# A mixer with chunked attention on one core: TensorE's instructions of batches 1 to 3 put in program order

## The chip, the cores and the metric

The kernel runs on one core of a Trainium2 chip. The metric is the time of one execution on the device, in microseconds. A core has five engines that run side by side, each with its own queue of instructions in a fixed order: PE (TensorE, matmuls; its weight loads are shown as PEld), DVE (VectorE), ACT (ScalarE), POOL (GpSimd) and SP (SyncE, which here issues DMAs). An instruction at the head of a queue waits on semaphores until what it needs is there, and everything behind it on that engine waits too.

## The reference

Four batches. Attention in chunks of 32 queries, each seeing 8 memory tokens and the keys from 16 ahead of the chunk to 8 behind it; then a mixer over tokens and over channels.

```python
for c in range(nc):                                   # q, k, v: 4 x 8 heads x 768 x 64, chunk 32
    k_full = concat(mem_k, k[:, :, l_start:r_end])     # 16 left, 8 right
    scores = scale * q_c @ k_full.T
    a = exp(scores - max(scores)); a = a / (sum(a) + 1e-09)
    out[:, :, c_start:c_end] = a @ v_full
...
x = out as [batch, 768, 512]
h = x.transpose(0, 2, 1) @ U @ V                       # rank 32, over tokens
u = x + h.transpose(0, 2, 1)
return u + relu(u @ w_ch1) @ w_ch2                     # 512 -> 2048 -> 512
```

## The kernel before

Everything is float32; TensorE multiplies in a format with fewer bits (fp32r), so each large operand is kept as two parts, high and low (names end in h and l: uh, ul, w1h, w1l, hh, hl), and a product is three passes. A batch has 768 tokens, two blocks of 384 (`blk`), each three tiles of 128 tokens (`TB`); the 2048 hidden channels are 16 groups `f` of 128 (`NF`).

The mixer of one block is a loop over f. `w1_step` (L1181) makes 12 matmuls of 128x384 into a PSUM bank ps_h: one group of hidden channels. ScalarE takes the relu as hh (L1189), VectorE the rest as hl (L1190). `w2_step` of the group before then adds to the three accumulators acc: six matmuls of 128x512 with hh (L1235), then three with hl (L1241). At the end `add_to_x` (L1197) adds acc to the tile x, which is sent out.

Batch 0 decodes the weights and does both blocks together; batch 1 is `ffn`, once for each block, and meanwhile makes sums of pieces of w1 (`keep_sums`, on POOL and DVE) and stores them (`save_sums`). Batches 2 and 3 are `sevens`: for each of 8 pairs of f, seven products of sums of w1 with sums of the turned tokens (six matmuls of 128x384 each, L1108, numbered 0 to 6) take the place of the eight w1 half steps; the sums of w1 come back by DMA, three ahead (`RING`). Results that are needed twice are kept by ScalarE (`keep`, L1129) and added to by VectorE (L1125). `hst` holds block 1's hidden groups, whose w2 steps end the batch with no products beside them. The turned tokens that the products take are made by `seven_u`: x is transposed on TensorE (L1049), copied (uc), and combined into bh/bl (products 0 and 1), t12h/t12l (2, 3), t34h/t34l (4, 5) and b22 (6), by casts on ACT (L1055) and subtractions on DVE (L1042; ta and tb are between).

The attention of batch b+1 runs during the mixer of batch b. It is a Python generator, `attention`, that yields after each "piece": loads, transposes of k and q (L484), 128x128 into ps_a; scores (L547), 64 small matmuls of 32x64 by 64 in the code and 128 in the trace, since a full float32 matmul is two instructions on the chip; exponentials (pt), their transposes (L601), the product with V (L620, "av", again 128 in the trace); tokens are three tiles T of 256. `regroup` (L433) lays out kn and qn on DVE for the transposes; `load_v` fills vb (L466, L473). After the last tile come U and V (L649, L877, L894).

What sets the order. A context `tc.manual_schedule(engines=FRONT)` with FRONT holding PE leaves TensorE's instructions in the order in which the code emits them. Before, it is opened ahead of batch 0 and closed in `following_pair`, at that batch's end. After that a scheduler, which simulates the engines, chooses among the instructions that its model finds ready; `tc.high_priority` draws some ahead. The order so chosen is fixed when the kernel is built. How many pieces have been emitted at which step of the mixer is set by `pcs` and `give()` (40 pieces), but on TensorE the scheduler puts their instructions where it will. Tile pools: a tag names a slot in SBUF, and whoever takes it next waits until its last reader is done. `up` holds uh and ul of the two blocks (tags uh, ul, uh1, ul1) and is closed, with the other pools of `plain`, by `other_pools()` between batches 1 and 2; the pools of `seven_u` take their room.

## Time and profile before

| | |
|---|---|
| three runs | 688.34, 688.49, 689.48 us; median 688.49 |
| profiled execution | 690.57 us, span 688.7 us, mean granted TensorE clock 0.987 |
| PE busy | 652.6 us, 95% of the span |
| PEld, DVE, ACT, POOL busy | 82%, 50%, 34%, 9% |
| chain that ended last | PE 84%, DVE 5%, SP's queue 4%, DMA 4% |

The profile is of one execution; its span goes from the first to the last instruction. In its rows L12 is line 12 of the kernel, out<-in names the tiles, and xN counts instructions. A row's duration is that of one instruction from issue to result; matmuls are pipelined, so that one which starts every 0.175 us lasts 0.34. What an instruction costs in a row of others is therefore read from starts, not from durations. Behind a row in brackets stands the idle time of its engine before it and what ended that. Lines move by the change: L1181 becomes L1205, L1108 becomes L1134, L1235 and L1241 become L1256 and L1262, L547, L601, L620 become L545, L599, L618, L484 becomes L486, L1042 and L1055 become L1054 and L1069, L1190 becomes L1214, L1197 becomes L1221.

### The profile page before, as it was taken

How to read it: one execution, taken by the hardware profiler on the slowest of the kernel's cores; microseconds unless marked ns; L12 is line 12 of the kernel's file. 1: busy time of each engine (PE TensorE's matmuls, PEld its weight loads, DVE VectorE, ACT ScalarE, POOL GpSimd, SP SyncE). 2: the span in 40 equal slices, each digit the busy share in tenths (PEclk: the TensorE clock that was granted, in tenths of full speed). 3: DMA queues.
4: the chain of work that ended last, by engine and by line, in shares of the span. 5: the costliest groups of instructions: out<-in, count | busy, mean ns of one | idle time of the engine just before them, and what ended most of it. 6: DMA issues, size and time to landing. Idle time of an engine off the chain costs nothing.

```text
span 688.7 us, 15153 instructions
## 1 busy us (share of the span) xinstructions
PE 652.6 (95%) x6184; PEld 562.0 (82%) x6188; DVE 344.9 (50%) x681; ACT 232.7 (34%) x574; POOL 63.0 (9%) x95
## 2 busy tenths in 40 slices
PE   7686999998998899999999979999999999999997
PEld 4455999997877599888879969898878889899886
DVE  5857787899454532436433463253256731222322
ACT  4525335335521234333221433333224621112221
POOL 2000000022003033302431100000000000000000
PEclk9998999999999999999999999999999999999999
DMA  8888354453571398564744547767533125556301
GB/s 233 151 253 285 116 190 154 163 151 116 124 145 34 125 321 240 156 178 147 205 131 154 170 148 230 188 181 189 149 112 108 32 71 173 167 143 168 124 11 46
DMA packets 121548, 106.37 MB, mean 154 GB/s; under 512 B 51240, under 2 KB 91048, under 8 KB 121480
## 3 DMA queue, kind: packets, MB, share of 16 engines
q1 hardware_dynamic: 121480, 105.41, 52.6%
q8 instruction: 49, 0.80, 0.5%
q14 instruction: 19, 0.16, 0.1%
HBM read 79.30 MB, written 25.17 MB: 152 GB/s over the span
## 4 chain that ended last, share of the span: by engine, by line
PE 84%; DVE 5%; SPq 4%; DMA 4%; issue 2%; ACT 1%; DVEq 0%; ACTq 0%
PE acc L1235 22%; PE ps_h L1181 18%; PE ps_h L1108 18%; PE acc L1241 11%; DMA rw<-in_moe_w_ch_dram 3%; PE ps_a L484 2%; PE ps_a L620 2%; PE ps_a L547 2%; PE ps_a L1235 2%; SPq L466 1%; PE ps_a L601 1%; PE acc L1227 1%; SPq L298 1%; DVE x L1197 1%; PE ps_a L649 1%
## 5 line engine op out<-in xcount | busy, mean ns | idle before, releaser
L1235 PE MATMUL acc<-w,hh 128*128 128x512 f32 x606 | 160.1, 397 | 0.0
L1235 PEld LDWEIGHTS acc<-w,hh 128*128 128x128 f32 x606 | 111.6, 189 | 21.9 <-issue 1.8
L1181 PE MATMUL ps_h<-uh,w1h 128*128 128x384 f32 x252 | 86.7, 348 | 7.3 <-ACT w1h L338 6.6
L1241 PE MATMUL acc<-w,hl 128*128 128x512 f32 x303 | 88.0, 395 | 0.0
L1181 PE MATMUL ps_h<-ul,w1h 128*128 128x384 f32 x252 | 85.4, 341 | 0.1
L1190 DVE SCALAR_TENSOR_TENSOR hl<-ps_h,hh 128x384 fp32r<-128x384 f32 x63 | 34.9, 553 | 89.9 <-ACT hh L1189 89.8
L1189 ACT ACTIVATE hh<-ps_h 128x384 fp32r<-128x384 f32 x63 | 30.9, 490 | 120.3 <-PE ps_h L1181 120.2
L1241 PEld LDWEIGHTS acc<-w,hl 128*128 128x128 f32 x303 | 56.1, 188 | 10.6
L1181 PE MATMUL ps_h<-uh,w1l 128*128 128x384 f32 x252 | 56.3, 345 | 0.0
L1181 PEld LDWEIGHTS ps_h<-uh,w1h 128*128 128x128 f32 x252 | 47.5, 190 | 10.5 <-ACT w1h L338 6.9
L1181 PEld LDWEIGHTS ps_h<-ul,w1h 128*128 128x128 f32 x252 | 47.9, 190 | 2.9 <-DVE ul L979 0.4
L1181 PEld LDWEIGHTS ps_h<-uh,w1l 128*128 128x128 f32 x252 | 46.0, 192 | 0.0
L1125 DVE TENSOR_TENSOR hst<-ps_h,hst 128x384 f32<-128x384 f32 x32 | 17.8, 556 | 47.8 <-ACT hst L1129 44.8
L1108 PE MATMUL ps_h<-t34h,w1l 128*128 128x384 f32 x128 | 39.8, 352 | 0.0
L1108 PE MATMUL ps_h<-t12h,w1l 128*128 128x384 f32 x128 | 38.3, 355 | 0.0
L1108 PE MATMUL ps_h<-bh,w1l 128*128 128x384 f32 x128 | 36.9, 341 | 0.0
L1125 DVE TENSOR_TENSOR c<-ps_h,c 128x384 f32<-128x384 f32 x16 | 8.9, 556 | 49.4 <-PE ps_h L1108 49.4
L1118 DVE SCALAR_TENSOR_TENSOR hl<-hst,hh 128x384 fp32r<-128x384 f32 x32 | 17.7, 555 | 30.4 <-PE acc L1241 27.7
L1129 ACT COPY hst<-ps_h 128x384 f32<-128x384 f32 x32 | 15.3, 478 | 45.5 <-PE ps_h L1108 45.5
L1117 ACT ACTIVATE hh<-hst 128x384 fp32r<-128x384 f32 x32 | 16.8, 525 | 40.8 <-PE acc L1235 34.5
L1001 POOL TENSOR_TENSOR vb<-w1h,w1l 128x512 f32<-128x512 f32 x16 | 20.7, 1299 | 91.7 <-DMA w1l<-w1ld 89.3
L1108 PEld LDWEIGHTS ps_h<-t34h,w1l 128*128 128x128 f32 x128 | 23.6, 188 | 4.3 <-ACT hst L1129 2.5
(233 smaller groups left out, 1090.5 us busy)
## 6 DMA issues: line engine op xcount, KB each, us to landing
w1l<-w1s SPq DMA_DIRECT2D x112, 256.0 KB
w1l<-w1ld SPq DMA_DIRECT2D x35, 256.0 KB
w1s<-sums SPq DMA_DIRECT2D x32, 256.0 KB
rw<-in_moe_w_ch_dram SPq DMA_DIRECT2D x14, 512.0 KB
qraw<-in_q_dram SPq DMA_DIRECT2D x24, 256.0 KB
out_dram<-x SPq DMA_DIRECT2D x24, 256.0 KB
vb<-in_v_dram SPq DMA_DIRECT2D x56, 98.0 KB
raw<-in_moe_w_ch_dram SPq DMA_DIRECT2D x20, 256.0 KB
```

The costliest lines, as they stand in the source:

```text
L484: nc.tensor.transpose(out=psv[:, p, r, :], in_=half[:, r, 2 * p:2 * p + 2, :].rearrange("n h d -> n (h d)"), identity=ident,)
L1001: nc.gpsimd.tensor_tensor(out=v2 if odd else v1, in0=hi, in1=lo, op=ALU.add)
L1108: nc.tensor.matmul(out=ps[:, :TOK], lhsT=w_, rhs=u, start=(start and m == 0), stop=(m == 5), skip_group_check=True,)
L1117: nc.scalar.activation(out=hh, in_=c, func=AF.Relu)
L1118: nc.vector.scalar_tensor_tensor(out=hl, in0=c, scalar=0.0, in1=hh.bitcast(F32), op0=ALU.max, op1=ALU.subtract,)
L1125: nc.vector.tensor_tensor(out=out, in0=ps[:, :TOK], in1=in1, op=ALU.add)
L1129: nc.scalar.copy(out=out, in_=ps[:, :TOK])
L1181: nc.tensor.matmul(out=ph[:, :TOK], lhsT=w[:, c, :], rhs=u[c], start=(m == 0), stop=(m + 1 == len(parts)),)
L1189: nc.scalar.activation(out=hh, in_=ph[:, :TOK], func=AF.Relu)
L1190: nc.vector.scalar_tensor_tensor(out=hl, in0=ph[:, :TOK], scalar=0.0, in1=hh.bitcast(F32), op0=ALU.max, op1=ALU.subtract,)
L1235: nc.tensor.matmul(out=acc[tt], lhsT=h[:, sl], rhs=w, start=(begins and m == 0), stop=False,)
L1241: nc.tensor.matmul(out=acc[tt], lhsT=hl[:, sl], rhs=w2h[f], start=False, stop=ends is not None)
```

## The change

The number of instructions on each engine stays the same; their order changes, most of all on TensorE. The manual order is closed at the end of the kernel, so the order of batches 1 to 3 is that of the code too. Pieces are given by `pace(slots)`: one call of `give` after each w1 step and one inside each w2 step, between the six hh and the three hl matmuls (ffn, 55 slots), six calls a pair in `sevens` (52 slots). There are 49 pieces in place of 40; some of the added ones hold no instruction. `seven_u` and the making of uh and ul (`uT_parts`) become generators, whose steps are given after the attention's pieces (`coming`). The pool `up` stays open; bh and bl, and the first two tiles hst, take the slots of uh, ul, uh1 and ul1. tb is made directly behind ta. The sums of w1 in batch 1 are made in the other of the two blocks for each pair of f.

Cut to its core:

```diff
+NPIECE = 49
...
+    up = ctx.enter_context(tc.tile_pool(name="up", bufs=1))
     plain = ExitStack()
-    up = plain.enter_context(tc.tile_pool(name="up", bufs=1))
...
+                regroup(kraw, kn, "kn", 0)
+                yield
+                for n, _ in enumerate(zip(load_parts(1), turns(0))):
+                    if n == 3:
+                        regroup(kraw, kn, "kn", 1)
                     yield
...
     def seven_u(b):
-        pool = seven["u"]
-        half = lambda name: pool.tile([P, NCK, TOK], F32R, name=name)
-        bh, bl = half("bh"), half("bl")
+        half = lambda pool, name, tag: pool.tile([P, NCK, TOK], F32R, name=name, tag=tag)
+        bh, bl = half(up, "bh", "ul"), half(up, "bl", "uh")
...
+        for tt, sl in enumerate(cols):
+            with tc.high_priority(offset=HIGH):
                 c0.append(turned_x(0, tt))
                 parted(bh[:, :, sl], bl[:, :, sl], c0[tt])
+            yield
+        for tt, sl in enumerate(cols):
+            with tc.high_priority(offset=HIGH):
                 c1.append(turned_x(1, tt))
                 ta.append(slot([P, NCK, P], F32, "ta"))
...
+                tb.append(slot([P, NCK, P], F32, "tb"))
+                sub(tb[tt][:, a], c1[tt][:, z], c1[tt][:, a])
+                sub(tb[tt][:, z], c0[tt][:, z], ta[tt][:, z])
+            yield "turned"
+        with tc.high_priority(offset=HIGH):
+            if "u" not in seven:
+                other_pools()
+            pool = seven["u"]
...
             product(xb, 7 * p + 2, False)
             keep(c12, xb)
+            give()
             product(yb, 7 * p + 3, True)
             give()
             product(xb, 7 * p + 4, False)
...
-            w2_step(b, 0, 2 * p, 0, p == 0, None, *h1)
+            w2_step(b, 0, 2 * p, 0, p == 0, None, *h1, give)
...
-            if b + 1 == SEVEN and f // 2 % 2 == blk:
+            if f // 2 % 2 != blk:
+                if f % 2 == 0:
+                    save_sums()
                 keep_sums(f, w1l)
             elif f % 2:
                 save_sums()
-            for _ in range(pieces[f]):
-                next(gen[0], None)
+            give()
...
-                w2_step(b, blk, *prev)
+                w2_step(b, blk, *prev, give)
...
+    def pace(slots):
+        tried, given = [0], [0]
+
+        def give():
+            tried[0] += 1
+            if tried[0] > slots:
+                next(coming[0], None)
+                return
+            while given[0] < NPIECE * tried[0] // slots:
+                next(gen[0], None)
+                given[0] += 1
+
+        return give
...
-            manual.close()
...
+        coming[0] = seven_u(b + 1) if b + 1 < B else iter(())
...
+    manual.close()
```

Three places show what becomes of the order. The first is on TensorE, in batch 2, at the scores of the next batch's first tile (kall, qt), among the products (ps_h) and w2 steps (acc). Before:

```order
L547 MATMUL ps_a<-kall,qt 32x64 x3
L1108 MATMUL ps_h<-b_4896,w1l 128x384 x6
L547 MATMUL ps_a<-kall,qt 32x64 x12
L1235 MATMUL acc_5066<-w_1354,hh 128x512 x2
L1235 MATMUL acc_5067<-w_1354,hh 128x512 x2
L1235 MATMUL acc_5068<-w_1354,hh 128x512 x2
L547 MATMUL ps_a<-kall,qt 32x64
L1241 MATMUL acc_5066<-w_1354,hl 128x512
```

After:

```order
L1134 MATMUL ps_h<-t12l,w1l 128x384
L1134 MATMUL ps_h<-t12h,w1l 128x384 x2
L545 MATMUL ps_a<-kall,qt 32x64 x64
L1134 MATMUL ps_h<-t34h,w1l 128x384
L1134 MATMUL ps_h<-t34l,w1l 128x384
```

The 64 small matmuls of a tile's scores (128 in the trace), of which 3, 12 and 1 are seen here between larger ones, now stand in one row. Over batch 2 the scores stood in 14 such groups and av in 7, and now each in three; in batch 1 they stood in five and four, and now in three and three.

The second place is TensorE at the turn from batch 1 to batch 2: the last w2 steps of batch 1 (w2last) and products 0 to 3 of batch 2. Before:

```order
L1241 MATMUL acc_4167<-w2last,hl 128x512
L1235 MATMUL acc_4165<-w2last,hh 128x512 x2
L1235 MATMUL acc_4166<-w2last,hh 128x512 x2
L1235 MATMUL acc_4167<-w2last,hh 128x512 x2
L1108 MATMUL ps_h<-bh,w1l 128x384
L1241 MATMUL acc_4165<-w2last,hl 128x512
L1241 MATMUL acc_4166<-w2last,hl 128x512
L1241 MATMUL acc_4167<-w2last,hl 128x512
L1108 MATMUL ps_h<-bh,w1l 128x384
L1108 MATMUL ps_h<-bl,w1l 128x384
```

After:

```order
L1262 MATMUL acc_4188<-w2last,hl 128x512
L1256 MATMUL acc_4186<-w2last,hh 128x512 x2
L1256 MATMUL acc_4187<-w2last,hh 128x512 x2
L1256 MATMUL acc_4188<-w2last,hh 128x512 x2
L1262 MATMUL acc_4186<-w2last,hl 128x512
L1262 MATMUL acc_4187<-w2last,hl 128x512
L1262 MATMUL acc_4188<-w2last,hl 128x512
L1134 MATMUL ps_h<-bh,w1l 128x384
L1134 MATMUL ps_h<-bl,w1l 128x384
```

Products now begin behind the whole of the last w2 step, whose hl matmuls the queue reaches first; products 2 and 3 with t12 stand at the same distance behind.

The third is VectorE there. Before:

```order
L1042 TENSOR_TENSOR t12l<-ta,t12h 128x4x128 x2
L1042 TENSOR_TENSOR b_4896<-uc,b_4896 128x2x128
L1197 TENSOR_TENSOR x<-acc_4165,x 128x512
L1042 TENSOR_TENSOR b_4896<-uc,b_4896 128x2x128
L1197 TENSOR_TENSOR x<-acc_4166,x 128x512
L1042 TENSOR_TENSOR b_4896<-uc,b_4896 128x2x128
L1197 TENSOR_TENSOR x<-acc_4167,x 128x512
L1042 TENSOR_TENSOR t34l<-tb,t34h 128x4x128 x2
L1042 TENSOR_TENSOR t12l<-ta,t12h 128x4x128
```

After:

```order
L1054 TENSOR_TENSOR t12l<-ta,t12h 128x4x128 x3
L1054 TENSOR_TENSOR t34l<-tb,t34h 128x4x128 x2
L1054 TENSOR_TENSOR b_4954<-uc,b_4954 128x2x128 x2
L1054 TENSOR_TENSOR t34l<-tb,t34h 128x4x128
L1054 TENSOR_TENSOR b_4954<-uc,b_4954 128x2x128
L1214 SCALAR_TENSOR_TENSOR hl<-ps_h,hh 128x384
L1221 TENSOR_TENSOR x<-acc_4186,x 128x512
```

The third t12l, for which TensorE waited, now comes directly behind the other two; the last hl of batch 1 stands behind all nine subtractions, where it had stood ahead of them.

## The prediction

> **What bounds the kernel.** I read the page's totals and slices first, then the chain of waits, then busy times by stage, and last the timeline of TensorE inside the two stages that the change rewrites. From the page (engine totals; TensorE's slices and its granted clock; the chain by engine):

> ```profile
> PE 652.6 (95%) x6184; PEld 562.0 (82%) x6188; DVE 344.9 (50%) x681; ACT 232.7 (34%) x574; POOL 63.0 (9%) x95
> ...
> PE   7686999998998899999999979999999999999997
> PEclk9998999999999999999999999999999999999999
> ...
> PE 84%; DVE 5%; SPq 4%; DMA 4%; issue 2%; ACT 1%; DVEq 0%; ACTq 0%
> ```

> TensorE is busy for 95% and is 84% of the chain; the next engine, VectorE, is at half. The busy time by stage (window, length, busy time of PE, PEld, DVE, ACT, POOL with instruction counts, granted clock, DMA share, GB/s) shows batch 0, batch 1, the turn from batch 1 to 2, batch 2, and the rest:

> ```profile
> 0.00:232.10 232.10, 205.30 (x2476) 171.57 (x2481) 161.62 (x309) 94.53 (x241) 21.83 (x45) 0.97 0.56 157
> 236.10:397.60 161.50, 161.09 (x1568) 142.72 (x1569) 68.14 (x146) 51.73 (x136) 40.56 (x48) 1.00 0.62 190
> 397.60:409.50 11.90, 8.10 (x32) 6.90 (x31) 8.20 (x16) 3.44 (x7) 0.00 (x0) 0.86 0.43 114
> 409.50:549.00 139.50, 139.50 (x1439) 119.38 (x1438) 64.68 (x137) 51.42 (x126) 0.61 (x2) 1.00 0.55 155
> 549.00:688.70 139.70, 135.98 (x665) 120.12 (x663) 38.26 (x69) 28.78 (x59) 0.00 (x0) 1.00 0.38 111
> ```

> In batch 2 TensorE is never idle, so nothing can be had there by waiting less. But busy is not the same as moving at full rate, and the timeline shows where it does not. Start, duration, engine, line, tile: an iteration of batch 1 with nothing in it, then one with the 128 scores in a row, then one with the 128 products by V (av) in a row:

> ```profile
> 241.94 0.34 PE L1181 MATMUL ps_h<-uh,w1h 128*128 128x384 f32 x1
> 242.12 0.34 PE L1181 MATMUL ps_h<-ul,w1h 128*128 128x384 f32 x1
> ...
> 246.10 0.34 PE L1181 MATMUL ps_h<-uh,w1h 128*128 128x384 f32 x1
> ...
> 274.96 0.34 PE L1181 MATMUL ps_h<-uh,w1h 128*128 128x384 f32 x1
> ...
> 277.16 1.49 PE L547 MATMUL ps_a<-kall,qt 64*32 64x64 f32 x128
> ...
> 280.75 0.34 PE L1181 MATMUL ps_h<-uh,w1h 128*128 128x384 f32 x1
> ```

> The empty iteration takes 246.10 - 241.94 = 4.16 us: 12 matmuls every 0.175 us (242.12 less 241.94, rounded) and 9 every 0.227. With one run of 128 scores it takes 5.79, so that run costs 1.63.

> **The change, term by term.**

> Term 1, fewer fragments. Where the scheduler cuts the same scores up in batch 2, the timeline reads:

> ```profile
> 443.80 0.34 PE L1108 MATMUL ps_h<-bh,w1l 128*128 128x384 f32 x1
> ...
> 444.95 0.31 PE L547 MATMUL ps_a<-kall,qt 64*32 64x64 f32 x6
> 445.19 0.44 PE L1108 MATMUL ps_h<-bh,w1l 128*128 128x384 f32 x1
> 445.47 0.34 PE L1108 MATMUL ps_h<-bl,w1l 128*128 128x384 f32 x1
> ...
> 446.42 0.89 PE L547 MATMUL ps_a<-kall,qt 64*32 64x64 f32 x68
> 447.25 0.45 PE L1108 MATMUL ps_h<-t12h,w1l 128*128 128x384 f32 x1
> ```

> From 443.80 to 445.19 lie six large matmuls (1.05) and the six small ones (what the trace counts; the code's small matmuls are two each): 0.34 too much, and the matmul behind them takes 0.28 to the next instead of 0.175, another 0.105. So six small ones cost 0.445, and 128 in a row cost 1.63: a line through both is 0.387 for the switch and 9.7 ns for each small matmul. The run of 68 tests it: 447.25 - 445.19 - 6 x 0.175 - 0.105 + 0.105 (its own late successor) = 1.01, and the line gives 1.05. A run thus costs some 0.385 whatever its length. By the orders, batch 2 has its scores in 14 fragments and its av in 7; batch 1 has 5 and 4, since transposes stand inside. After, there are three and three in each: 15 + 3 = 18 fewer, 18 x 0.385 = 6.9. Bounds: 7.7 with the whole 0.43 that a run of two costs, and 0 if the cuts only fill holes (a rival). I take 6.9.

> Transposes go the other way: by the orders of batches 1 to 3, 13 joints between groups of four are opened. Two groups side by side, and then one, cost

> ```profile
> 250.94 0.34 PE L1181 MATMUL ps_h<-uh,w1h 128*128 128x384 f32 x1
> ...
> 256.01 0.34 PE L1181 MATMUL ps_h<-uh,w1h 128*128 128x384 f32 x1
> ...
> 260.64 0.34 PE L1181 MATMUL ps_h<-uh,w1h 128*128 128x384 f32 x1
> ```

> 5.07 - 4.16 = 0.91 for two and 4.63 - 4.16 = 0.47 for one: a joint saves 0.03, not 0.385, so opening 13 costs +0.4 (the bounds are 0 and 13 x 0.105 = 1.4, where each pays a whole late successor).

> Term 2, the turn from batch 1 to batch 2. TensorE, and VectorE at the same time:

> ```profile
> 400.08 0.44 PE L1108 MATMUL ps_h<-t12h,w1l 128*128 128x384 f32 x1
> 404.22 0.63 PE L1108 MATMUL ps_h<-t12l,w1l 128*128 128x384 f32 x1 [3.69 <-DVE t12l L1042]
> ...
> 407.80 1.54 PE L1235 MATMUL acc<-w,hh 128*128 128x512 f32 x6
> ```

> ```profile
> 397.94 0.42 DVE L1042 TENSOR_TENSOR tb<-uc,ta 128x256 f32<-128x256 f32 x1
> 398.27 1.28 DVE L1042 TENSOR_TENSOR t12l<-ta,t12h 128x512 fp32r<-128x512 f32 x2
> 399.48 0.42 DVE L1042 TENSOR_TENSOR b<-uc,b 128x256 fp32r<-128x256 f32 x1
> ```

> Product 1's 12 matmuls take 7.72 us here instead of 2.10, 5.6 too much; with the restarts ahead of it (395.4 to 400.1) I count 6.15. Of that 3.69 is the wait for the last t12l, and about 1.6 the matmuls behind it, eleven at 0.32 instead of 0.175. In the stretch behind the wait the granted clock is 0.53:

> ```profile
> 404.20:407.80 3.60, 3.58 (x11) 3.58 (x12) 1.60 (x3) 1.00 (x2) 0.00 (x0) 0.53 0.16 24
> ```

> [...]

> After, bh and bl lie in the pool that stays open, so products 0 and 1 no longer wait behind w2's last step. What is late next: VectorE now has three t12l, three t34l and three b22 ahead of the last hl (L1214), which w2's last step waits for, and TensorE waits in order. From the third tile's transposes to the need of hl lie 3 x 0.227 + 2.10 + 2.04 + 1.36 = 6.2 us of matmuls; VectorE needs, by spacing in its rows, 4 x 0.33 + 3 x 0.605 + 3 x 0.605 + 3 x 0.34 = 6.0, with ScalarE's copy (about 0.6) ahead and hl (0.55) behind, 7.1. So about 0.9 stays, with 0.5 for restarts 1.4. Bounds: 0.35 (no stall) and 4.15 (ta waits for slots that the stores of the sums free). I take 1.4: -4.75, range -2.0 to -5.8.

> Term 3, product 5 of each pair. Before, it stands behind only three w2 matmuls (0.68 us), while ScalarE must have emptied its bank:

> ```profile
> 576.87 0.86 PE L1241 MATMUL acc<-w,hl 128*128 128x512 f32 x3
> 577.60 0.44 PE L1108 MATMUL ps_h<-t34h,w1l 128*128 128x384 f32 x1
> 577.88 0.34 PE L1108 MATMUL ps_h<-t34l,w1l 128*128 128x384 f32 x1
> ```

> It starts 0.73 behind the first of them, 0.05 late, and its first matmul takes 0.28, 0.10 late: 0.15 for each of batch 3's 8 pairs, 1.2. After, all nine w2 matmuls stand there, 2.04 us. I take -1.1, between 0 and -1.2; in batch 2 most pairs have attention there, which term 1 has priced. Five products in a row also ask for their sums faster; I cost that at nothing: three sums are fetched ahead, and each product of cover is 1.05 us; without the cover it would be one wait of term 5's size.

> Term 4, the turn from batch 0 to 1: VectorE bound, as it stays; two g,v matmuls come later, out of a wait into the path: +0.2.

> Term 5, new waits. A fixed order waits where the scheduler would have put something else. Batch 0, already in a fixed order, shows the price, at its av runs:

> ```profile
> 196.67 0.92 PE L620 MATMUL ps_a<-vb,pT 64*32 64x64 f32 x62 [1.06 <-issue]
> 210.51 0.83 PE L620 MATMUL ps_a<-vb,pT 64*32 64x64 f32 x62 [1.05 <-issue]
> 214.05 0.45 PE L620 MATMUL ps_a<-vb,pT 64*32 64x64 f32 x28 [0.90 <-issue]
> ```

> ```profile
> L473 SPq DMA_DIRECT2D vb<-in_v_dram x4: 393/1046/1365, 180.0 to 204.1; - x4
> ```

> There the last loads of V are issued at 204.1, 5 to 10 us ahead of the last two waits. In the new order 18 to 22 us of matmuls stand between V's loads and the av run, so few such waits should come. Bounds: 0 (it cannot be below nothing, as the stretch of batch 2 has no idle to save) and twice batch 0's 3.0, 6.0. I take 1.5, half of one such set.

> What else moves costs nothing by its cover: the regrouping of q and k one piece earlier, and tb ahead of t12l, on VectorE at half load; the loads of q, k and V on SP's queue, with the DMA share at 0.55 in batch 2; the sums on POOL, at 9%, made in the other block of batch 1. Without that cover each would cost one piece's wait, about 1 us, and that is in term 5.

> Sum: -6.9 + 0.4 - 4.75 - 1.1 + 0.2 + 1.5 = -10.65. The profiled execution took 690.57 (span 688.70 and 1.87 around it), so 679.9; it stands 2.08 above the median of the three runs, 688.49. Against the median: **677.8 us**.

> **Rivals.**

> The other side: the fixed order waits. If each of the six score and six av runs, and the four or so transposes behind each exponential, waits once as in batch 0, at 1.05, ten waits undo the gain and more make it slower: 16 waits cost 16.8, less 12.15 of gains (the sum without term 5), 693.1. It decides at 12. Against it: V's lead of 18 us above. For it: batch 0, in a fixed order, is busy only 205.3 of 232.1, though its first part waits for weights. I give slower 0.11, and 0.19 to a middle case of 4 to 9 waits: 680 to 686.

> The cuts filled holes: where small matmuls stand between products, TensorE would otherwise have waited for a bank to be emptied. Then term 1 is nothing, and 684.7 follows. Against it: batch 3's products have no small matmuls between them and lose 0.15 a pair, not 0.385 a cut. I give 0.08, within the middle case's span.

> The clock falls in long runs. If 128 small matmuls did not count as work, each of the new whole runs would be followed by a slow stretch like that above, 1.6 us. The new order has 12 whole runs, of which 4 stood before: 8 x 1.6 = 13 us, so 690, no gain. Against it, the window of one of the four (the clock stands behind the five busy times):

> ```profile
> 276.90:278.60 1.70, 1.70 (x131) 1.35 (x129) 0.56 (x1) 0.71 (x2) 0.00 (x0) 1.00 0.50 55
> ```

> The clock stays at 1.00, and the large matmuls behind that run keep their rate (the iteration of 5.79), and so I give this 0.02. [...]

> The turn does not get shorter: if ta waits for its slots, term 2 is -2.0, 680.5; this lies in the forecast's own range.

> **How the numbers follow.** About 0.2% (1.4 us) is what a measurement of this kernel can tell from no change. Forecast, 673.5 to 680.5: 0.55. Middle case (waits or holes), 680.5 to 687: 0.27. The clock, 690: 0.02, half within 0.2%. Waits short of the whole gain, 687.1 to 689.9: 0.05. Slower by waits: 0.11. So faster 0.82, same 0.06, slower 0.12. The low end, 673.5, is the sum with term 1 at 7.7, term 2 at 5.8 and no waits (674.5), less 1.0 for sizes rounded in the rows; the high end, 687, takes in the middle case, and what is left out is 0.18 above and 0.02 below. The forecast's own range is 673.5 to 680.5.

> **What would show it.** Term 1: the timeline has L545 and L618 as x128 in one row each, and the stage from the turn to the end of batch 2 is some 5.5 us shorter with the same instructions. Term 2: the wait of 3.69 on t12l is gone, a wait of about 1 us on hl stands ahead of w2's last step in batch 1, and the clock there stays at 1.00. Term 3: product 5's first row in batch 3 reads 0.34. Term 5: the waits of TensorE have few new lines on L599, L618 or L545 in batches 1 and 2. The prediction is wrong if these waits sum to over 5 us, or if L1134 shows starts late by more after the runs were joined than before.

## The result, and the profile after

The changed kernel takes 682.13 us, median of 17 runs (678.34 to 685.91), against 689.48 for the kernel before in 17 runs beside them; the ratio is 0.9892, 95% interval 0.9869 to 0.9914. The forecast was 677.8, with a range of 673.5 to 687.0: faster, as forecast, by 7.4 us where 10.65 was forecast. The profiled execution took 685.91 us, the longest of the 17, which matters below.

The page's totals and chain read almost as before: the same 6184 matmuls, busy for the same share.

```profile
PE 648.7 (95%) x6184; PEld 563.7 (82%) x6188; DVE 345.2 (50%) x681; ACT 234.7 (34%) x574; POOL 63.0 (9%) x95
...
PE 86%; DVE 5%; SPq 3%; DMA 2%; issue 2%; ACT 1%; ACTq 0%; DVEq 0%
```

The list of TensorE's waits (what waited and for what: us in total, times, longest) no longer has the 3.7 on t12l; four of its lines are new or longer:

```profile
PE ps_h L1134 <- DMA w1l<-w1s: 2.5, 1, 2.5
...
PE ps_h L1205 <- DVE ul L997: 1.8, 1, 1.8
...
PE acc L1256 <- ACT hh L1213: 0.5, 1, 0.5
...
PE acc L1262 <- DVE hl L1214: 0.4, 1, 0.4
```

By stage (window, length, busy time of PE, PEld, DVE, ACT, POOL, clock, DMA share, GB/s): batch 0, batch 1, the turn from batch 1 to 2, the stretch behind it, the rest of batch 2, and the end.

```profile
0.00:233.10 233.10, 207.59 (x2476) 172.80 (x2481) 161.45 (x309) 94.50 (x241) 16.55 (x39) 0.96 0.55 156
237.00:396.40 159.40, 159.40 (x1558) 141.85 (x1559) 70.70 (x150) 54.27 (x141) 45.83 (x54) 0.99 0.63 191
396.40:412.00 15.60, 14.71 (x72) 12.52 (x71) 8.64 (x18) 3.62 (x9) 0.00 (x0) 1.00 0.59 180
412.00:419.00 7.00, 4.52 (x20) 4.04 (x19) 0.55 (x2) 0.48 (x1) 0.00 (x0) 0.78 0.91 249
419.00:545.00 126.00, 126.00 (x1390) 110.62 (x1390) 61.42 (x131) 51.58 (x123) 0.61 (x2) 1.00 0.54 144
545.00:683.80 138.80, 135.07 (x669) 121.16 (x667) 38.56 (x70) 28.62 (x59) 0.00 (x0) 0.99 0.38 116
```

The turn no longer holds an idle stretch of nearly 4 us. The next window does: 412 to 419 has 4.52 us of work in 7.00, at a clock of 0.78, with the DMA share at 0.91. That is a loss that the kernel before did not have.

To compare stages exactly, I number the 2592 large matmuls (w1 steps, products, w2 steps) of each trace in order of start; both kernels run the same number of them. The table gives, for each stretch of numbers, its length in a kernel's trace less its length in the trace of the kernel before, in us. A to F are numbers 670 to 700 (the turn from batch 0 to 1), 700 to 1330 (batch 1), 1330 to 1390 (the turn from 1 to 2), 1390 to 1450 (the stretch behind it), 1450 to 2020 (the rest of batch 2), 2020 to the end. A stretch with attention in it also shifts where a piece moves over its border, so D and E are best read together. Up to number 670 the code is the same, and its length alone differs from that in the trace of the kernel before by -2.8 to +1.9 in these traces; that is left out, and it is why the medians of single experiments, 6 runs each, settle less than the traces do.

| kernel | A | B | C | D | E | F | sum | median us | ratio to before (95%) |
|---|---|---|---|---|---|---|---|---|---|
| changed (its profile) | +1.99 | -1.37 | -4.56 | +5.51 | -6.38 | -1.16 | -5.97 | 682.13 | 0.9892 (0.9869 to 0.9914) |
| changed, again | +0.42 | -1.47 | -4.48 | +3.44 | -6.41 | -1.15 | -9.65 | 681.99 | 0.9900 (0.9858 to 0.9941) |
| g,v put back | +0.45 | -2.01 | -4.69 | +6.08 | -6.44 | -1.15 | -7.76 | 681.57 | 0.9891 (0.9851 to 0.9931) |
| stores later | +3.10 | -1.53 | -4.84 | +1.46 | -5.42 | -1.10 | -8.33 | 679.01 | 0.9849 (0.9817 to 0.9882) |
| both mended | +0.43 | -2.00 | -4.50 | +1.28 | -6.43 | -1.15 | -12.37 | 679.53 | 0.9849 (0.9817 to 0.9880) |
| loads later | +0.44 | -1.53 | -4.91 | +1.17 | -4.75 | -1.07 | -10.65 | 677.64, one run | |
| loads later, g,v back | +0.46 | -2.02 | -4.91 | +1.55 | -4.25 | -1.17 | -10.34 | 679.92 | 0.9861 (0.9831 to 0.9892) |
| all three | +0.46 | -1.92 | -4.86 | +0.42 | -4.36 | -1.15 | -11.41 | 680.51 | 0.9851 (0.9813 to 0.9888) |
| scores cut | +0.43 | +0.93 | -4.85 | +5.09 | -1.56 | -1.11 | -1.07 | 689.59 | 0.9997 (0.9974 to 1.0021) |
| scheduler's order | +0.25 | -1.74 | -6.13 | +5.37 | -2.39 | +0.68 | -3.96 | 686.20 | 0.9942 (0.9920 to 0.9963) |
| before, stores later | 0.00 | +0.12 | +0.10 | 0.00 | -0.09 | -0.33 | -0.20 | 689.88, one run | |

In TensorE's timeline after, the scores of a tile stand in one row, product 5 of a pair in batch 3 starts at full rate behind its w2 step (0.18 to the next, where the first matmul took 0.28 before), and the last w2 step of batch 1 waits twice:

```profile
435.91 1.48 PE L545 MATMUL ps_a<-kall,qt 64*32 64x64 f32 x128
437.32 0.44 PE L1134 MATMUL ps_h<-t34h,w1l 128*128 128x384 f32 x1
437.60 0.34 PE L1134 MATMUL ps_h<-t34l,w1l 128*128 128x384 f32 x1
...
573.10 0.84 PE L1262 MATMUL acc<-w,hl 128*128 128x512 f32 x3
573.78 0.34 PE L1134 MATMUL ps_h<-t34h,w1l 128*128 128x384 f32 x1
573.96 0.34 PE L1134 MATMUL ps_h<-t34l,w1l 128*128 128x384 f32 x1
```

```profile
397.73 1.66 PE L1256 MATMUL acc<-w2last,hh 128*128 128x512 f32 x6 [0.48 <-ACT hh L1213]
399.75 0.96 PE L1262 MATMUL acc<-w2last,hl 128*128 128x512 f32 x3 [0.36 <-DVE hl L1214]
400.55 0.34 PE L1134 MATMUL ps_h<-bh,w1l 128*128 128x384 f32 x1
```

So the gains came, and two losses stand beside them, in A and in D.

### The profile page after: what moved, and what is told of

Its sections match the earlier page's. It is cut to its first block, busy times and chain, and to the rows that moved or that the text cites. A ratio compares the mean times of both kernels' runs of the same rounds, so it can differ in the third digit from the quotient of the medians.

```text
span 683.8 us, 15135 instructions
## 1 busy us (share of the span) xinstructions
PE 648.7 (95%) x6184; PEld 563.7 (82%) x6188; DVE 345.2 (50%) x681; ACT 234.7 (34%) x574; POOL 63.0 (9%) x95
## 4 chain that ended last, share of the span: by engine, by line
PE 86%; DVE 5%; SPq 3%; DMA 2%; issue 2%; ACT 1%; ACTq 0%; DVEq 0%
PE acc L1256 22%; PE ps_h L1205 19%; PE ps_h L1134 18%; PE acc L1262 11%; PE ps_a L618 2%; PE ps_a L486 2%; PE ps_a L545 2%; PE ps_a L1256 2%; PE ps_a L599 1%; PE acc L641 1%; PE acc L1250 1%; PE ps_a L908 1%; DMA w1l<-w1s 1%; PE ps_a L647 1%; PE ps_a L1262 1%
## 5 line engine op out<-in xcount | busy, mean ns | idle before, releaser
L1214 DVE SCALAR_TENSOR_TENSOR hl<-ps_h,hh 128x384 fp32r<-128x384 f32 x63 | 35.0, 555 | 88.5 <-ACT hh L1213 88.4
L1134 PE MATMUL ps_h<-t34h,w1l 128*128 128x384 f32 x128 | 39.4, 349 | 0.0
L1134 PE MATMUL ps_h<-bh,w1l 128*128 128x384 f32 x128 | 36.7, 346 | 2.5 <-DMA w1l<-w1s 2.5
L1134 PE MATMUL ps_h<-t12h,w1l 128*128 128x384 f32 x128 | 37.4, 347 | 0.0
L1143 ACT ACTIVATE hh<-hst 128x384 fp32r<-128x384 f32 x32 | 16.8, 525 | 36.8 <-PE acc L1256 32.4
L910 DVE TENSOR_TENSOR x<-ps_a,x 128x512 f32<-128x512 f32 x24 | 16.4, 689 | 23.1 <-PE ps_a L908 23.1
L1134 PEld LDWEIGHTS ps_h<-bh,w1l 128*128 128x128 f32 x128 | 24.0, 192 | 3.4 <-issue 2.8
```

The source lines that it names most:

```text
L910: nc.vector.tensor_tensor(out=x, in0=hp, in1=x, op=ALU.add)
L1134: nc.tensor.matmul(out=ps[:, :TOK], lhsT=w_, rhs=u, start=(start and m == 0), stop=(m == 5), skip_group_check=True,)
L1143: nc.scalar.activation(out=hh, in_=c, func=AF.Relu)
L1214: nc.vector.scalar_tensor_tensor(out=hl, in0=ph[:, :TOK], scalar=0.0, in1=hh.bitcast(F32), op0=ALU.max, op1=ALU.subtract,)
```

## The experiments

**The loss in D: a sum of w1 that lands late.** Timeline of TensorE, and of SP's issues, in the changed kernel:

```profile
413.09 0.51 PE L1134 MATMUL ps_h<-bh,w1l 128*128 128x384 f32 x2
416.09 0.66 PE L1134 MATMUL ps_h<-bh,w1l 128*128 128x384 f32 x1 [2.48 <-DMA w1l<-w1s]
416.54 0.52 PE L1134 MATMUL ps_h<-bl,w1l 128*128 128x384 f32 x1
416.86 0.52 PE L1134 MATMUL ps_h<-bh,w1l 128*128 128x384 f32 x1
```

```profile
406.35 0.35 SPq L1118 DMA_DIRECT2D w1l<-w1s  x1
406.79 1.39 SPq L1231 DMA_DIRECT2D out_dram<-x  x3
408.27 2.01 SPq L425 DMA_DIRECT2D qraw<-in_q_dram  x2
410.38 1.05 SPq L1118 DMA_DIRECT2D w1l<-w1s  x2
```

Product 1 of the second pair waits 2.48 us for its sum, and the matmuls behind it go at a clock of 0.50 (415.97 to 419.38; 0.32 from start to start, where full clock has 0.175). Its sum, the ninth, is the first of the two issued from 410.38: it stands behind three stores of x (768 KB), two loads of q (512 KB) and k, and takes until 416.1. Theory: the wait on t12l had given the queue time for this. The first edit takes only the stores out of the way:

```diff
-            send()
+            if p > 1:
+                send()
```

> The changed kernel with the last three stores of x of batches 1 and 2 (256 KB each) issued behind product 4 of the third pair instead of the first. Theory (the removed wait had given the DMA queue time to drain, and now products reach a sum of w1 that is behind k, q and the stores on the queue): 768 KB less ahead of it, at the 0.3 to 0.4 MB per us moved there, lands the sum 1.9 to 2.5 us earlier; the wait of 2.48 us on w1l<-w1s falls under 0.6 and the half clock behind it goes, 3.5 to 4.5 us in all. Rival (the sum is late because its own slot is freed late): the wait stays within 0.5 us of 2.48 and the time does not change.

Measured: D falls from +5.51 to +1.46, 4.05 us less, and by 2.0 against the changed kernel's second trace (3.44), in which the wait was 1.94 with no half clock behind it. The wait on the ninth sum is gone, and with it the half clock. The 0.8 us on a sum that the list of waits still has (0.75 at 432.01) is another one, 18 us later, in E, and E is 1.0 worse (-5.42 against -6.38); in the second trace with this edit (both mended) there is none, and why it is here was not followed up. The ninth sum is issued 2 us earlier, 5.4 us ahead of the product that takes it, where it had been 3.2:

```profile
406.90 0.35 SPq L1118 DMA_DIRECT2D w1l<-w1s  x1
407.35 0.94 SPq L425 DMA_DIRECT2D qraw<-in_q_dram  x2
408.38 1.67 SPq L1118 DMA_DIRECT2D w1l<-w1s  x2
```

The rival falls, and the theory holds for this wait. But the stores had cost in two ways, the time in which SP issues them (1.39 us in the row at 406.79) and their 768 KB, and this run changes both. Two more runs ask whether it is the bytes or the stores as such, and whether the kernel before pays for them. In the first, `give()` is left out at three places of pair 0 and the stores stay:

```diff
-            give()
+            if p > 0:
+                give()
```

> The changed kernel with the first three pieces of attention in batch 2 (loads of k and q) three places later, the stores left where they are. Theory (what counts is the bytes ahead of the sum on the queue): 512 to 1024 KB less ahead of it, 1.4 to 2.5 us, so the wait of 2.5 us on w1l<-w1s is under 1 us and the half clock behind it is gone. Rival (only the stores matter, since they wait for the last adds to x on VectorE and hold up the queue of issues): the wait stays above 2 us.

The wait is 0.6 us, D is +1.17:

```profile
404.26 0.98 SPq L1118 DMA_DIRECT2D w1l<-w1s  x2
```

```profile
408.18 0.41 PE L1134 MATMUL ps_h<-bh,w1l 128*128 128x384 f32 x1 [0.57 <-DMA w1l<-w1s]
```

Here the ninth sum is issued 3.4 us ahead of its need, hardly more than the 3.2 of the changed kernel, but it is there 3.9 us after its issue, not 5.7 (5.1 in the second trace, 6.4 in the one with g,v put back): the bytes ahead of it count by themselves. But E is worse by 1.6 (-4.75 against -6.38). Of that 0.5 is an idle stretch ahead of scores at 459.7; the rest was not followed up.

The second is the kernel before, with the stores later:

> The kernel before with the last three stores of x of batches 1 and 2 issued two pairs later. Theory (before, the 3.7 us wait on t12l at the turn covers the queue, so that no product waits for its sums): the turn and the start of batch 2 keep their length within 0.5 us. Rival (the stores cost time there whatever stands before them): 2 us or more shorter.

C and D change by 0.1 and 0.0 us, as the theory had it. The rows of the kernel before say how the old wait covered the queue:

```profile
408.43 1.39 SPq L1207 DMA_DIRECT2D out_dram<-x  x3
409.92 0.55 SPq L423 DMA_DIRECT2D qraw<-in_q_dram  x1
410.56 0.76 SPq L1092 DMA_DIRECT2D w1l<-w1s  x1
```

```profile
415.97 0.69 PE L1108 MATMUL ps_h<-bh,w1l 128*128 128x384 f32 x3
416.50 0.34 PE L1108 MATMUL ps_h<-bl,w1l 128*128 128x384 f32 x1
```

The ninth sum is issued at 410.56 there, and the product that takes it begins with the third of the row's three matmuls, at 416.3, 5.8 us later. After, it is issued at almost the same time, 410.38, but TensorE, no longer held at t12l, is there at 413.6. Before, the sum was in time; now TensorE waits for the queue.

**The loss in A: two matmuls taken out of a hole.** In the changed kernel the first matmuls of batch 1 stand so (timeline, then two windows with their clock, the third number from the end):

```profile
234.75 0.44 PE L1205 MATMUL ps_h<-uh,w1h 128*128 128x384 f32 x1 [0.67 <-ACT uh L996]
237.00 0.44 PE L1205 MATMUL ps_h<-ul,w1h 128*128 128x384 f32 x1 [1.81 <-DVE ul L997]
...
239.46 0.53 PE L1205 MATMUL ps_h<-uh,w1h 128*128 128x384 f32 x1
239.78 0.53 PE L1205 MATMUL ps_h<-ul,w1h 128*128 128x384 f32 x1
```

```profile
235.07:238.48 3.41, 1.59 (x9) 1.48 (x9) 1.88 (x4) 0.00 (x0) 0.00 (x0) 1.00 0.97 348
238.48:241.89 3.41, 3.41 (x13) 3.41 (x12) 0.56 (x1) 0.49 (x1) 3.25 (x4) 0.50 0.90 224
```

Before, two g,v matmuls stood within the wait for ul:

```profile
234.75 1.10 PE L894 MATMUL ps_a<-g,v 96*128 96x512 f32 x2 [0.44 <-DVE ul L979]
```

The edit in `w1_step` puts them back:

```diff
+            if m == 0 and (b, blk, f) == (1, 0, 0):
+                next(late[0])
+                next(late[0])
```

> The changed kernel with two g,v matmuls put back behind the first matmul of batch 1, where the scheduler had them. Theory (the split idle time kept the clock): in the changed kernel TensorE stands idle 0.67 and 1.81 us at that turn and then runs some 3 us at a granted clock near 0.5; with the two matmuls in the hole the clock stays at 1.00 there and the stage from the last w2 step of batch 0 to the second w1 step of batch 1 is 1.5 to 2.0 us shorter. Rival (the two matmuls cost only their own 0.23 us each wherever they stand): the slow stretch stays and the stage is 0.2 to 0.5 us shorter.

In the trace, the clock stays at 1.00 and A is +0.45:

```profile
231.12 0.44 PE L1205 MATMUL ps_h<-uh,w1h 128*128 128x384 f32 x1 [0.68 <-ACT uh L996]
232.17 1.10 PE L908 MATMUL ps_a<-g,v 96*128 96x512 f32 x2 [0.61 <-DVE ul L997]
233.37 0.45 PE L1205 MATMUL ps_h<-ul,w1h 128*128 128x384 f32 x1
```

The median, 681.57, does not show it: the edit costs or gains less than its interval. What it wins in every trace lies in B: -2.01 here, and -1.92 to -2.02 in the other three traces with the two matmuls put back, against -1.37 to -1.53 where they stand later in batch 1. That is 0.5 us, close to the 0.23 us that each of the two takes. The repeat of the changed kernel tells why.

> The changed kernel itself on the same chip, as the measure for the other three. From the runs so far: 682 us, ratio 0.989. In its profile the wait on w1l<-w1s of 2.0 to 3.0 us in batch 2 must be there again (it follows from the order of the DMAs), while the stretch at half clock behind the turn from batch 0 to 1 may be there or not, if it depends on where a window of the clock's control falls.

It has the same 1.81 us of idle time, no slow stretch, and A of +0.42, as much as with the edit:

```profile
232.99 0.44 PE L1205 MATMUL ps_h<-uh,w1h 128*128 128x384 f32 x1 [0.68 <-ACT uh L996]
235.24 0.44 PE L1205 MATMUL ps_h<-ul,w1h 128*128 128x384 f32 x1 [1.81 <-DVE ul L997]
```

```profile
233.72:237.13 3.41, 1.89 (x11) 1.89 (x12) 1.47 (x3) 0.00 (x0) 0.30 (x1) 1.00 0.89 317
237.13:240.55 3.42, 3.42 (x20) 3.21 (x19) 1.25 (x2) 0.79 (x2) 3.34 (x4) 1.00 0.85 247
```

So the slow stretch is not in every execution. Of the seven traces with the two matmuls out of the hole (those of the two earlier cuts of the scores, named below, among them), three have it (A from 1.99 to 3.11) and four do not (0.42 to 0.44); of the seven with them in it, the two of the kernel before among these, none. Where the stretch is there, it costs 1.6 to 2.7 us, more than the expected 1.5 to 2.0.

The half clock behind the wait in D came and went in the same way: it is there behind 2.48 us in the profile (1.04 us of work in its window), behind 2.96 us with g,v put back and 2.03 us with the scores cut (1.38 and 1.39), and not behind the 1.94 us of the second trace, which two windows share (2.44 and 2.45). Some work in a window did not prevent it: half clock came behind windows with up to 1.84 us of work.

**Both mended.** The two edits together:

> The changed kernel with both edits: two g,v matmuls back behind the first matmul of batch 1, and the three stores issued two pairs later. Theory (the two losses are separate and each is mended by its own edit): the turn from batch 0 to 1 reads as in the kernel before within 0.6 us, the wait on w1l<-w1s is gone, and the time is 5 to 6 us under the changed kernel, 675.5 to 678, ratio to before 0.980 to 0.984. Rival (one loss hides the other, or a third wait takes their place): 679 to 682.

Measured: A +0.43, D +1.28, no wait on a sum in the list, and a sum over the stages of -12.37. The two losses are separate in the trace. The median, 679.53, is 2.5 us under the changed kernel, but over the 678 expected and within the 679 to 682 of the rival, though no third wait is seen in the trace, which is of the fastest of the six executions (676.68); so by time the 5 to 6 us are not shown. The interval of its ratio, 0.9817 to 0.9880, overlaps the changed kernel's only from 0.9869 on. Later loads in place of later stores, and then all three edits:

> The changed kernel with the first loads of k and q in batch 2 three places later and the two g,v matmuls back in the turn from batch 0 to 1. Theory: the two losses add up, 676.5 to 678.5, ratio 0.980 to 0.983. Rival (later loads make the attention late and its pieces wait): 679.5 or more.

> The same with the three stores two pairs later as well. Theory (the queue is no longer late, so there is nothing more to win): within 0.6 us of the kernel with later loads and g,v. Rival (the 0.6 us that the sum is still waited for with later loads goes too, with its restart): 0.6 to 1.2 us less.

They give 679.92 and 680.51, the same as both mended within their intervals. The first missed its 678.5 and lies where its rival had it; E is -4.25 there, with an idle stretch of 0.6 us ahead of scores. Stores later alone, 679.01, is as good: of the mended versions none can be told from another by time.

**The price of a cut.** Each of the six score runs in batches 1 and 2 is cut into four, with every other matmul in its place:

```diff
+                    if cutting[0] and (t, p) != (1, NPR - 1) and p % 2:
+                        yield "cut"
```

> The changed kernel with each of its six score runs of batches 1 and 2 in four pieces of 16 matmuls (32 in the trace), two large matmuls apart or one, and every other matmul of TensorE in exactly the order of the changed kernel: 18 more pieces. Theory (0.385 us a piece): batches 1 and 2 together 6.9 us longer. Rival (pieces fill holes): under 1.5 us. If scores that end later are waited for as well, more than 6.9, with new waits on pt.

(Two earlier forms of this cut, 691.67 and 691.64 us, let later pieces of the attention slip, so that part of the turned tokens was taken from x ahead of its last sums; their times are not used, and of their traces only the turn from batch 0 to 1, which lies ahead of the cuts.) Measured: 689.59 against 681.99, and in the traces B to E are 6.4 to 8.5 us longer, 6.9 if the wait in D, which varies, is left out (-5.48 for B, C and E against -12.31 and -12.36). The rival, that cuts fill holes, falls. But the agreement with 6.9 is partly chance: 2.2 us are new waits on pt in batch 2, since the scores end later.

```profile
PE ps_a L610 <- ACT pt L582: 2.2, 2, 1.3
```

```profile
434.06 0.45 PE L545 MATMUL ps_a<-kall,qt 64*32 64x64 f32 x32
434.44 0.45 PE L1152 MATMUL ps_h<-t34h,w1l 128*128 128x384 f32 x1
434.73 0.33 PE L1152 MATMUL ps_h<-t34l,w1l 128*128 128x384 f32 x1
434.99 0.46 PE L545 MATMUL ps_a<-kall,qt 64*32 64x64 f32 x32
```

From 434.06 to 434.99 stand one piece of 32 and two large matmuls: 0.93 - 2 x 0.175 = 0.58 for the piece. A whole run costs, in the changed kernel, 437.32 - 435.91 = 1.41 and 0.105 for the late successor, 1.515. Four pieces of 0.58 make 2.32, so three more cost 0.80, 0.27 each: less than the 0.385 of the pieces between whole products from which the forecast was made. 18 x 0.27 = 4.8 and 2.2 of waits make 7.0, near the 6.9. Batch 1, which has no new wait, says the same: B is 2.3 to 2.4 us longer for nine more pieces, 0.26 each.

**The scheduler's order with all else changed.** The manual order is closed at the end of batch 0 again, pools and pieces as changed:

```diff
         late[0] = chain(gen[0], uT_parts(1, 1))
+        manual.close()
```

> The changed kernel with the manual order closed at the end of batch 0 as before; pools, pieces and loads as changed. Its order has scores in 11 and av in 9 pieces in batch 2 instead of three and three, and whole runs in batch 1. Theory (the gain is the joined runs and product 5's place; the turn from batch 1 to 2 is short thanks to the pool): 14 more pieces, 5.4 us, and 1.1 us for product 5, so 4 to 8 us slower than the changed kernel in batches 2 and 3, while the wait on t12l stays away. Rival (the order as such does nothing, the pool and the places of the pieces do it all): within 1.5 us of the changed kernel.

Measured: 686.20, 4.1 us over the changed kernel, at the low end of what was expected. C is -6.13: the short turn comes from the pool and from where the turned tokens are made, not from TensorE's program order. D has the late sum (+5.37, a wait of 1.67) without the new order too. E loses 4.0 against the changed kernel, with 14 more pieces (0.29 each, if it is all theirs), and F 1.8: what stood well in batch 3, product 5 among it, needs the fixed order. The rival, that the order as such does nothing, falls.

## Why the prediction was right, and where it was off

Term 1 (-6.9 for 18 fewer pieces, +0.4 for opened transposes): right. B, D and E together are -7.15 where the sums do not wait (both mended); the second trace of the changed kernel, less its 1.94 of wait, gives -6.4, or -6.9 without the 0.5 for the two g,v matmuls that stand in its batch 1. This contains product 5 in batch 2, which was not priced, so the pieces are worth somewhat less than 0.385 each, as the cut shows (0.26 to 0.27). The forecast for both, -6.5, lies within 0.7 of these numbers, and as product 5 is in them, part of that is luck.

Term 2 (-4.75 at the turn): right, -4.5 to -4.9 in the table's traces with the new order. (The twelve matmuls that the prediction calls product 1's are those of products 2 and 3, with t12; its sum is not touched by that.) The forecast counts on the 1.6 us of slow matmuls behind the old wait going whole; no run shows that a shorter wait does this, and it was the author's estimate. What the runs show: the waits that stay are 0.48 on hh and 0.36 on hl, where 0.9 was worked out, and the clock is 1.00 there; but half clock came behind waits of 2.03 to 2.96 us in D, which are shorter than the old one of 3.69 too.

Term 3 (-1.1): -1.15, with the row of product 5 at full rate.

Term 4 (+0.2 at the turn from batch 0 to 1): too small, and the step that failed is that moving the two g,v matmuls would cost no more than their time. Their time is 0.5, in B. A itself is +0.42 to +0.46 with them put back as without, where the clock holds: by the timelines the second matmul with uh, 0.18, had stood ahead of the wait for ul, and one g,v matmul, 0.25, now stands ahead of the first w2 step. And A is +2.0 to +3.1 where the clock falls, in three of the seven traces with the two matmuls out of the hole: half clock stands behind a window with 1.59 us of work in the profile of the changed kernel, and none behind 1.89 in the repeat.

Term 5 (1.5 for new waits): the size was too small and the place was wrong. None of the av runs waited in batch 1 or 2. The step that failed is in term 3: the faster demand for sums was costed at nothing, with the three sums fetched ahead as the cover. The three are fetched ahead in program order, but each issue stands in SP's queue behind stores and loads of other work. The 1.28 MB of stores and q ahead of the ninth sum would take about 5 us at the 249 GB/s of that window, and TensorE is there 3.2 us after the issue. The loss is 2.2 us (3.44 less the 1.28 of both mended) without the half clock and 4.2 with it (5.51 less 1.28).

Together: -5.97 to -9.65 over the stages in two traces, -7.4 in the medians, against -10.65; with both losses mended the stages give -12.37, where the terms without term 5 were -12.15; the medians of both mended differ by less, 10.8 us. The rivals of waiting and of holes lose (no waits in batches 1 and 2 but the one; the cut), and the clock did not fall in the long runs:

```profile
435.90:437.40 1.50, 1.50 (x130) 1.40 (x129) 0.00 (x0) 0.22 (x1) 0.00 (x0) 1.00 0.66 175
```

## What to carry to other kernels

A long wait at a turn between stages can also be time that the DMA queue uses, as the 3.69 us on t12l were: with it the ninth sum was issued 5.8 us ahead of its product, without it 3.2, and TensorE waited 2.48. Before counting the removal of such a wait as gain, list what is issued there and how many bytes stand ahead of the first transfer that the next stage needs, and move stores that nobody waits for out of the way. When small work is moved out of a wait, look at what it leaves: one longer hole can cost more than the work, as here, where two matmuls of 0.23 us each left a hole of 1.81 us and, in three of seven traces, a stretch at half clock that cost 1.6 to 2.7. And a run of small matmuls had a price of its own each time it was cut, 0.26 to 0.27 us here, which is read from starts, not from busy time.

## What had not been expected of the hardware

Half clock behind short idle time: with 0.67 and 1.81 us of it, one matmul apart, in three of seven traces of the same order, and behind single waits of 2.03 to 2.96 us but not behind one of 1.94. In these fourteen traces the work within windows of 3.41 us tells most of them apart: half clock each time behind 1.45 us or less, in none behind 1.85 or more, and either between. And the price of a change between small and large matmuls was 0.27 us in the cuts inside a product and 0.385 where it was read between products; that the place makes the difference was not tested.
